# A kernel's planner gets new constants for transfers and a new searched order (block attention and a SoLU layer, one core)

## The chip, the cores and the metric

The kernel runs on one core of one Trainium2 chip. Its engines are TensorE (PE, with a weight-load row PEld), VectorE (DVE), ScalarE (ACT), GpSimd (POOL) and SyncE (SP), which here only issues transfers. Times are device microseconds of one execution; lower is better. An engine executes its own instructions strictly in the order in which the program lists them, each after the semaphores that it needs.

## The reference

Four batches, eight heads, 768 positions, head size 64. Attention runs over a local band of keys and, beside it, over the maxima of blocks of 32 keys; the values are the rows and the block means. Its result goes, as 3072 rows of 512, into a layer with a SoLU and a norm.

```python
k_sum = k.reshape(B, H, nb, 32, D).max(axis=3)
v_sum = v.reshape(B, H, nb, 32, D).mean(axis=3)
scores_l = where(|i - j| < 16, scale * q @ k.T, -1e9)
scores_s = scale * q @ k_sum.T + log(32)
a = softmax(concat([scores_l, scores_s]))          # over both
x = (a @ concat([v, v_sum])) as rows of H * D       # 3072 x 512
h = x @ w_in                                        # 3072 x 1024
solu = h * softmax(h)
ln = (solu - mean) / sqrt(var + 1e-6) * g_ln
out = ln @ w_out                                    # 3072 x 512
```

## The kernel before, in words

The work is cut into 24 tiles t of 128 rows. For a tile, `scores` multiplies queries (qt) with copied windows of keys (kw, line 668), VectorE masks and takes maxima, ScalarE takes the exponentials, `values_turn` transposes them (line 723), and `values` multiplies with the value tile vt (line 770), which holds 96 rows of values (`load_v`) and 24 rows of block means (`load_v2` copies them from vsum). The result is split into a rounded part and a rest (xh, xl), so that three fast matmuls give one precise product. The first product with w_in is `first` (line 922) for the first 8 tiles; from tile 8 on `first_two` (line 941) computes two tiles at once from sums of quarters, with fewer matmuls. `solu` follows, and `second_parts` (line 1117) multiplies with w_out into banks o.

Between `solu` and the second product a tile has to be transposed. Tiles 6 to 23 are "far": `send` transposes 32x32 blocks on VectorE into the one buffer tbl (line 1047) and writes them to DRAM (farl<-tbl, line 1051), and `fetch` reads them back in four transfers of 128 KB (lt<-farl, line 1057), which puts the blocks where they belong. `rows_split` then rounds them on ScalarE or VectorE (lh, lines 367 and 368) and takes the rest (ll). All transfers but the stores of the result and a few copies are issued by SyncE, in one queue.

The order of instructions is not written by hand. The code lists over 1,800 operations, each with one or more engines that can do it, a price for each engine, and what it reads and writes. `Plan.order` plays them through: each engine takes the operation that can begin first, by due time where several can, and an operation with an alternative engine goes where it would end sooner. `Plan.issue` first sets the due times, adds the corrections of the table URGENT and the leanings of the table LEANING (which tilt the choice of an engine), and at the end emits the program in the planned order. While TensorE would stand idle before 80 us (FILL), it puts in dummy matmuls of zeros (line 1309). What the planner believes of a transfer is a few constants: it begins 1 us after its issue ends, all transfers queue one after another at the rate RATES, and it is readable LAND (or an operation's own `land`) after its last byte:

```python
                own = o.end + 1.0 + o.nbytes / self.SMALL * 1e-3
                dma += o.nbytes / next(r for t, r in self.RATES if dma <= t) * 1e-3
                o.end = (own if e == "act" else dma) + (0.2 if dma < self.LATE else o.land or self.LAND)
```

A transfer that moves slower than its bytes say is given more bytes: the write of a far tile counts 1.6 times (FARK), and so does the read back. The price of an operation in `op(engine, price, ...)` is what its engine is held for, for a transfer the time of its issue.

Of the kernel before, what the change touches and what calls it, by code (L numbers as in the profile page):

```python
# [20 lines left out]
P = 128  # L21
# [21 lines left out]
NEAR = 6  # L43
FAR_FROM = 6
FARS = 8
FARK = 1.6
FAR_TO = 24
LATER = 20
PAIRED = 8
# [35 lines left out]
class Plan:  # L85
# [4 lines left out]


    RATES = (6.9, 270.0), (30.0, 410.0), (60.0, 365.0), (1e9, 410.0)
    SMALL, LATE = 40.0, 50.0
    LAND = 2.2
    START = 0.7
    COLD, FILL = 6.9, 80.0
    IDLE = 0.22
    WAIT, FAR = 1.5, 200
    DEAR = {"dve": 1.0, "act": 0.3, "pool": 1.0}
    SYNC = 0.16  # L100
    URGENT = {0: -688, 1: -604, 2: -542, 3: -576, 4: -600, 5: -520, 6: -519, 7: -505, 8: -506, 9: -507, 10: -319, 11:
# [34 lines left out]
    LEANING = {88: -1.9, 97: 1.6, 106: 5.6, 112: -6.5, 157: -5.9, 172: 3.6, 229: 0.2, 294: 1.1, 296: 0.5, 305: -5.8,  # L136
# [8 lines left out]

    def __init__(self):
        self.ops, self.rings, self.banks, self.idle, self.slots = [], {}, {}, None, []
# [106 lines left out]
    def order(self):  # L254
# [45 lines left out]
        while len(order) < len(self.ops):  # L300
            t, e, o = min(((x[0], e, x[1]) for e in ready for x in [take(e)] if x),
                          key=lambda x: (x[0], x[2].due), default=(0.0, None, None))
            if o is None:
                return None
            for f in o.can:
                ready[f] = [x for x in ready[f] if x[1] is not o]
            then.pop(e, None)
            if o.then:
                then[e] = o.then
            o.start, o.engine, (o.cost, o.fn) = t, e, o.can[e]  # L310
            o.end = free[e] = t + cost(e, o, t)
            if e == "dve" and o.port:
                held = o.end
            if e == "pool" and o.port:
                lock = o.end
            if o.nbytes:
                dma = max(dma, o.end + 1.0)
                own = o.end + 1.0 + o.nbytes / self.SMALL * 1e-3
                dma += o.nbytes / next(r for t, r in self.RATES if dma <= t) * 1e-3
                o.end = (own if e == "act" else dma) + (0.2 if dma < self.LATE else o.land or self.LAND)  # L320
            order.append(o)
            for u in o.users:
                u.left -= 1
                if not u.left:
                    enter(u)
# [14 lines left out]
def attn_then_solu(ctx: ExitStack, tc: tile.TileContext, q, k, v, vr, vb, w_in, w_out, g_ln, out):  # L340
# [220 lines left out]
    def mean_values_pe(b):  # L561
# [16 lines left out]
        rows = plan.buf(sb, [P, DM], F32, "os", 2, f"vs{b}")  # L578
        op(act, 0.48, lambda: nc.scalar.copy(out=rows.ap, in_=to()), r=[acc], w=[rows])
        for g in range(4):  # L580
            op(act, 0.34, lambda g=g: nc.scalar.dma_start(
                out=y.ap[WIN + 6 * g:WIN + 6 * g + 6, :], in_=rows.ap[32 * g:32 * g + 6, :]),
               r=[rows], w=[(y, g)], nbytes=6 * 2048)

# [21 lines left out]
    def mean_values(b):  # L606

        vsum[b] = y = plan.buf(sb, [P, DM], F32, "vsum", 1, f"vsum{b}")
        for h in range(H):
            x, p0 = vacc[b, h // 4], h % 4 * NB  # L610
            op(sp, 0.43, lambda h=h, x=x, p0=p0: nc.sync.dma_start(
                out=y.ap[WIN:KC, h * D:(h + 1) * D], in_=x.ap[p0:p0 + NB, :]), r=[x], w=[(y, h)], nbytes=NB * 256)

    def load_q(b, g, pairs=None, after=()):
# [12 lines left out]

    def load_v2(b, g):
        x, y = vt[b, g], vsum[b]
        e, cost, queue = (sp, 0.43, nc.sync) if b else (act, 0.8, nc.scalar)  # L630
        return op(e, cost, lambda: queue.dma_start(
            out=x.ap[WIN:KC], in_=y.ap[WIN:KC, :].rearrange("p (o c) -> p o c", o=1).broadcast_to([NB, G, DM])),
            r=[y], w=[(x, 1)], nbytes=NB * 8192)

    def scores(b, g, pp, direct=False, each=False):

# [417 lines left out]
    def fetch(d, to):  # L1054

        for q in range(4):
            op(sp, 0.43, lambda q=q: nc.sync.dma_start(
                out=to.ap[32 * q:32 * q + 32],
                in_=d.ap.rearrange("(i b) (q x) -> q b i x", i=4, q=4)[q]), r=[d], w=[(to, q)], nbytes=int(P * DF * FARK))

    sent = {}

# [82 lines left out]
    for pp in range(NPP):  # L1145
# [1 line left out]
            key_blocks(0, p)  # L1147
        run(scores(0, 0, pp, True, True))
        if pp == 0:
            op(pool, 0.8, selector, w=[sel_b])  # L1150
            mean_values_first(0)
    for i in range(2 * NKC):
        split_w_in(*divmod(i, 2))
# [200 lines left out]
```

## Time and profile before

| | before |
|---|---|
| time, median of 3 runs | 365.95 us (363.23 to 366.72) |
| the profiled execution: its own time | 365.1 us |
| its span, first to last instruction | 363.4 us |
| granted TensorE clock, mean | 0.994 |
| busy: PE, DVE, ACT, POOL | 353.1, 303.3, 274.1, 170.1 us |
| moved by DMA | 68.19 MB |

The execution's own time has 1.7 us outside the span of its instructions. Busy TensorE is not TensorE at its peak: matmuls are pipelined, and a matmul that is slow to start counts as busy.

### The profile page before, as it was taken

The page shows a single profiled execution, that of the slowest core. Times are in us where ns is not written, and L with a number is a line of the kernel's source. Part 1 is how long each engine was busy: PE and PEld are TensorE (multiplying, and loading weights), DVE is VectorE, ACT ScalarE, POOL GpSimd, SP SyncE. Part 2 cuts the span into 40 slices and gives each one's busy share as a digit, 9 for nine tenths or more (in the row PEclk, how much of TensorE's full clock was granted, in tenths as well). Part 3 has the DMA queues.
Part 4 walks back from the last instruction along what each step waited for, and adds up shares of the span by engine and source line. Part 5 has one row for each costly group of instructions (what it writes and reads, how often), then busy time and mean ns, then how long its engine had stood idle before and what let it go on. Part 6 is the DMA issues. An engine that isn't in the chain of part 4 may idle for free.

```text
span 363.4 us, 9364 instructions
## 1 busy us (share of the span) xinstructions
PE 353.1 (97%) x3318; PEld 276.6 (76%) x3318; DVE 303.3 (83%) x965; ACT 274.1 (75%) x800; POOL 170.1 (47%) x304
## 2 busy tenths in 40 slices
PE   8799999899999999999799999999999999999996
PEld 3438667677777888888688888888888878888886
DVE  4989999998989999896799699895899978949530
ACT  4788999868988988898697597893796976745221
POOL 5542532448779786266636265352332114434400
PEclk9999999999999999999899999999999999999999
DMA  7999994155228047357595193394193282154531
GB/s 250 417 416 389 358 407 156 56 175 170 102 88 265 5 138 252 103 175 239 171 365 181 35 293 135 93 340 114 20 294 118 60 282 90 37 187 168 187 117 58
DMA packets 28530, 68.19 MB, mean 188 GB/s; under 512 B 3852, under 2 KB 13324, under 8 KB 26948
## 3 DMA queue, kind: packets, MB, share of 16 engines
q1 hardware_dynamic: 24620, 60.87, 49.5%
q10 hardware_dynamic: 3864, 6.74, 5.2%
q8 instruction: 26, 0.43, 0.5%
q14 instruction: 20, 0.16, 0.2%
HBM read 49.55 MB, written 15.73 MB: 180 GB/s over the span
## 4 chain that ended last, share of the span: by engine, by line
PE 85%; DMA 10%; DVE 2%; SPq 1%; ACT 1%; issue 0%; ACTq 0%
PE o L1117 33%; PE h L922 13%; PE hu L941 11%; PE x L770 6%; PE s L668 6%; PE hl L941 5%; DMA farl<-tbl 4%; PE t L723 4%; DMA st_v<-in_vr 3%; PE hf L941 2%; DMA raw<-in_w_in 2%; DMA lt<-farl 1%; PE vs_ps L555 1%; PE lt L723 1%; DVE tbl L1047 1%; PE x L762 1%
## 5 line engine op out<-in xcount | busy, mean ns | idle before, releaser
L1117 PE MATMUL o<-w,lh 128*128 128x512 f32 (+1 forms) x400 | 128.7, 385 | 0.7 <-DVE he L1012 0.7
L1117 PEld LDWEIGHTS o<-w,lh 128*128 128x128 f32 x400 | 74.1, 188 | 16.2 <-DVE he L1012 0.9
L1117 PE MATMUL o<-w,ll 128*128 128x512 f32 (+1 forms) x200 | 76.2, 381 | 0.0
L695 ACT ACTIVATE e<-e,nm 128x120 f32<-128x120 f32 x192 | 73.7, 392 | 0.0
L922 PE MATMUL h<-w,xh 128*128 128x512 f32 x128 | 44.2, 404 | 0.0
L1117 PEld LDWEIGHTS o<-w,ll 128*128 128x128 f32 x200 | 37.6, 188 | 6.8
L687 DVE CUSTOM_DVE_ANT_0 e<-s,mask 128x120 f32<-128x120 f32 x192 | 40.6, 277 | 0.4 <-PE s L668 0.4
L695 ACT ACTIVATION_READ_ACCUMULATOR e<-e,nm 128x1 f32 x192 | 37.6, 196 | 0.0
L375 POOL TENSOR_TENSOR ll<-lt,lh 128x512 fp32r<-128x512 f32 x16 | 21.7, 1359 | 29.0 <-DVE lh L368 15.1
L1004 ACT ACTIVATE he<-hs,hm 128x512 f32<-128x512 f32 x24 | 17.2, 718 | 18.0 <-DVE hm L994 18.0
L367 ACT CAST lh<-lt 128x512 fp32r<-128x512 f32 x34 | 20.0, 608 | 14.2 <-PE o L1117 10.5
L1031 POOL TENSOR_SCALAR ss<-ss 128x1 f32<-128x1 f32 x24 | 7.7, 322 | 49.2 <-ACT sq L1027 48.7
L922 PEld LDWEIGHTS h<-w,xh 128*128 128x128 f32 x128 | 24.0, 187 | 7.0 <-DVE nmu L1015 0.8
L1047 DVE STREAM_TRANSPOSE tbl<-he 128x1024 f32<-128x1024 f32 x18 | 22.3, 1237 | 8.2 <-DMA farl<-tbl 7.9
L770 PEld LDWEIGHTS x<-at,vt 120*64 120x64 f32 (+1 forms) x768 | 25.1, 142 | 4.6 <-issue 2.7
L770 PE MATMUL x<-at,vt 120*64 120x64 f32 (+1 forms) x768 | 27.2, 228 | 0.0
L1027 ACT ACTIVATE sq<-he 128x1024 bf16<-128x1024 f32 x24 | 25.4, 1057 | 1.6 <-DVE z L701 1.4
L367 ACT COPY at<-t 120x512 f32<-120x512 f32 x40 | 21.3, 590 | 6.8 <-PE t L723 6.8
L369 POOL COPY kw<-ksum 128x192 f32<-128x192 f32 x19 | 8.4, 441 | 36.0 <-PE s L668 33.6
L922 PE MATMUL h<-w,xl 128*128 128x512 f32 x64 | 25.0, 391 | 0.0
L668 PE MATMUL s<-kw,qt 64*64 64x120 f32 x704 | 22.4, 273 | 2.1 <-ACT kw L367 2.1
L374 DVE TENSOR_TENSOR e<-e,z 128x960 f32<-128x960 f32 x20 | 23.4, 1172 | 0.2
(176 smaller groups left out, 851.5 us busy)
## 6 DMA issues: line engine op xcount, KB each, us to landing
vt<-in_v SPq DMA_DIRECT2D x12, 1024.0 KB
farl<-tbl SPq DMA_DIRECT2D x18, 512.0 KB
lt<-farl SPq DMA_DIRECT2D x72, 128.0 KB
kraw<-in_k SPq DMA_DIRECT2D x16, 400.0 KB
out<-os ACTq DMA_DIRECT2D x23, 256.0 KB
qt<-in_q SPq DMA_DIRECT2D x11, 512.0 KB
raw<-in_w_in SPq DMA_DIRECT2D x8, 512.0 KB
raw<-in_w_out SPq DMA_DIRECT2D x8, 512.0 KB
```

Source lines behind the costliest of these rows:

```text
L367: by = {act: lambda: nc.scalar.copy(out=to(), in_=of()), dve: lambda: nc.vector.tensor_copy(out=to(), in_=of()), pool: lambda: nc.gpsimd.t ...
L374: by = {dve: lambda: nc.vector.tensor_tensor(out=to(), in0=a(), in1=b(), op=kind), pool: lambda: nc.gpsimd.tensor_tensor(out=to(), in0=a() ...
L375: pool: lambda: nc.gpsimd.tensor_tensor(out=to(), in0=a(), in1=b(), op=kind)}
L668: nc.tensor.matmul(sc.ap[cu * QT:(cu + 1) * QT, j, c:c + ks.shape[-1]], qs.ap[ds, 2 * pp + i, u * QT:(u + 1) * QT], ks, start=True, stop=True)
L687: nc.vector.tensor_tensor_reduce(out=e.ap[:, n, :], in0=sc.ap[:, j, (2 * i + up) * KC:(2 * i + up + 1) * KC], in1=mask[:, mi, :], scale=-S ...
L695: nc.scalar.activation(out=e.ap[:, n, :], in_=e.ap[:, n, :], func=AF.Exp, bias=nm.ap[:, n:n + 1], scale=-1.0, accum_out=z.ap[:, n:n + 1])
L770: nc.tensor.matmul(xp()[j * D:(j + 1) * D, i, qs], vs.ap[:k, u, cs], at.ap[:k, u % 2, n[j] + u // 2, :], start=not apart, stop=not apart o ...
L922: nc.tensor.matmul(hp.ap, a.ap[:, c, ts], w.ap[:, i], start=(c == 0 and n == 0), stop=(c == NKC - 1 and n == 2))
L941: nc.tensor.matmul(to.ap, operand(y, n)[:, c], w(c).ap(i), start=first and c == 0 and k == 0, stop=c == 1 and k == 2, skip_group_check=True)
L1027: op(act, 1.06, lambda: nc.scalar.activation(out=sq.ap, in_=e.ap, func=AF.Square, accum_out=ss.ap), r=[e], w=[sq, ss])
L1047: op(dve, 1.17, lambda: nc.vector.transpose(out=tb.ap.rearrange("p (q c a) -> p q c a", q=4, a=32), in_=of().rearrange("p (c q a) -> p q c ...
L1117: nc.tensor.matmul(o.ap[:, cols], a.ap[:, f, :], w.ap[:, i, cols], start=(f == 0 and n == 0), stop=(f == NFC - 1 and n == 2))
```

## The change

No operation is added or removed, and no operand is changed: the same operations are planned with other prices and other tables. After it

- the landing constant depends on when the transfer ends: 0.5 us up to 15 us, 1.4 up to 50, 1.9 later, instead of 0.2 up to 50 and 2.2 later; an operation's own `land` now counts at all times;
- the read back of a far tile counts 2.3 times its bytes, instead of 1.6; the write stays at 1.6 with a landing of 0.1;
- the copy of block means into a value tile for batches 1 to 3 holds SyncE 0.86 us and counts four times its bytes, instead of 0.43 and once;
- the sixteen copies vsum<-vacc hold SyncE 0.76 us each instead of 0.43, the four copies vsum<-vs hold ScalarE 0.75 each instead of 0.34;
- the selector on GpSimd is priced 1.6 us instead of 0.8;
- URGENT and LEANING are replaced. They come from a search whose measure is the mean of five replays of the plan, some of them with disturbances.

```diff
-FARK = 1.6
+FARK, BACK = 1.6, 2.3
...
-    SMALL, LATE = 40.0, 50.0
-    LAND = 2.2
+    SMALL = 40.0
+    LANDS = (15.0, 0.5), (50.0, 1.4), (1e9, 1.9)
...
-    URGENT = {0: -688, 1: -604, 2: -542, 3: -576, 4: -600, 5: -520, 6: -519, 7: -505, 8: -506, 9: -507, 10: -319, 11:
...
+    URGENT = {0: -1754, 1: -1655, 2: -1738, 3: -1698, 4: -1638, 5: -1639, 6: -1608, 7: -1510, 8: -1410, 9: -1372, 10:
...
-    LEANING = {88: -1.9, 97: 1.6, 106: 5.6, 112: -6.5, 157: -5.9, 172: 3.6, 229: 0.2, 294: 1.1, 296: 0.5, 305: -5.8,
...
+    LEANING = {81: 0.8, 100: -4.4, 109: -11.8, 172: 24.7, 176: -6.4, 280: -7.8, 294: -11.9, 296: -5.6, 305: -18.3,
...
-                o.end = (own if e == "act" else dma) + (0.2 if dma < self.LATE else o.land or self.LAND)
+                o.end = (own if e == "act" else dma) + (o.land or next(x for t, x in self.LANDS if dma <= t))
...
-            op(act, 0.34, lambda g=g: nc.scalar.dma_start(
+            op(act, 0.75, lambda g=g: nc.scalar.dma_start(
...
-            op(sp, 0.43, lambda h=h, x=x, p0=p0: nc.sync.dma_start(
+            op(sp, 0.76, lambda h=h, x=x, p0=p0: nc.sync.dma_start(
...
-        e, cost, queue = (sp, 0.43, nc.sync) if b else (act, 0.8, nc.scalar)
+        e, cost, queue = (sp, 0.86, nc.sync) if b else (act, 0.8, nc.scalar)
...
-            r=[y], w=[(x, 1)], nbytes=NB * 8192)
+            r=[y], w=[(x, 1)], nbytes=NB * 8192 * (4 if b else 1))
...
-                in_=d.ap.rearrange("(i b) (q x) -> q b i x", i=4, q=4)[q]), r=[d], w=[(to, q)], nbytes=int(P * DF * FARK))
+                in_=d.ap.rearrange("(i b) (q x) -> q b i x", i=4, q=4)[q]), r=[d], w=[(to, q)], nbytes=int(P * DF * BACK))
...
-            op(pool, 0.8, selector, w=[sel_b])
+            op(pool, 1.6, selector, w=[sel_b])
```

## Rows read from the trace of the kernel before

**Rows 1.** The page: the span, and the busy time of each engine with its share of the span and its instructions.

```profile
span 363.4 us, 9364 instructions
PE 353.1 (97%) x3318; PEld 276.6 (76%) x3318; DVE 303.3 (83%) x965; ACT 274.1 (75%) x800; POOL 170.1 (47%) x304
```

**Rows 2.** The table by stretches of 20 us: the stretch and its length, then busy us and instructions of PE, PEld, DVE, ACT, POOL, the granted clock, the share of DMA, GB/s. Of the eight stretches from 180 to 340 us the first and the one in which PE is least busy are shown.

```profile
20.00:40.00 20.00, 20.00 (x237) 13.01 (x236) 18.80 (x56) 17.07 (x48) 6.48 (x15) 1.00 1.03 385
40.00:60.00 20.00, 20.00 (x202) 13.48 (x201) 19.70 (x68) 18.94 (x60) 6.43 (x11) 1.00 0.93 355
60.00:80.00 20.00, 18.97 (x202) 13.97 (x200) 19.63 (x51) 15.53 (x40) 9.00 (x13) 1.00 0.30 87
...
160.00:180.00 20.00, 17.94 (x162) 14.55 (x163) 14.28 (x58) 15.41 (x53) 13.43 (x24) 0.95 0.65 209
180.00:200.00 20.00, 20.00 (x167) 16.79 (x164) 18.77 (x55) 17.50 (x58) 11.05 (x22) 0.96 0.77 269
...
280.00:300.00 20.00, 19.59 (x206) 16.04 (x203) 18.00 (x69) 17.81 (x61) 2.85 (x7) 1.00 0.47 156
```

**Rows 3.** The dummy matmuls alone (line 1309): the first stretch of 20 us and the sum over all stretches in the same table (PE, PEld), and from the list of that line's instructions (min/median/max ns, first and last start) the form that comes last.

```profile
0.00:20.00 20.00, 11.60 (x45) 4.56 (x45) 1.00 0.91 340
...
sum 363.40, PE 17.00 PEld 6.36; mean PE 0.94 PEld 0.35
...
L1309 PE MATMUL x<-zero x8: 379/379/390, 24.2 to 77.0; 128*128 128x512 bf16 x8
```

**Rows 4.** What TensorE waited for: us in total, times, the longest.

```profile
PE s L668 <- ACT kw L367: 2.1, 1, 2.1
PE vs_ps L1309 <- DVE zero L392: 1.2, 1, 1.2
...
PE o L1117 <- DVE he L1012: 0.7, 1, 0.7
PE s L668 <- DMA kraw<-in_k: 0.6, 1, 0.6
PE s L668 <- DMA qt<-in_q: 0.6, 1, 0.6
```

**Rows 5.** The chain of work that ended last, from 140 to 185 us: start, us, what.

```profile
156.06 1.80 PE s L668 x64
157.86 2.04 PE x L770 x64
...
170.16 5.38 DMA lt<-farl
...
176.34 0.74 ACT kw L367
...
177.13 2.58 PE s L668 x64
179.71 2.86 PE x L770 x64
```

**Rows 6.** ScalarE in order of time: start, us, what, and the idle time before it with what ended it.

```profile
175.72 0.62 ACT L367 CAST lh<-lt 128x512 fp32r<-128x512 f32 x1 [1.93 <-DMA lt<-farl]
```

**Rows 7.** The table by stretches, four us at a time, with the columns of rows 2.

```profile
174.00:178.00 4.00, 1.94 (x38) 1.44 (x40) 2.74 (x6) 1.35 (x2) 1.58 (x2) 1.00 0.24 95
178.00:182.00 4.00, 4.00 (x92) 3.70 (x86) 3.99 (x38) 3.72 (x13) 3.67 (x13) 0.57 0.62 167
```

**Rows 8.** SyncE's queue in order of time: start, us, what, how many.

```profile
167.36 0.34 SPq L1057 DMA_DIRECT2D lt<-farl  x1
167.80 0.86 SPq L631 DMA_DIRECT2D vt<-vsum  x1
168.72 2.43 SPq L1057 DMA_DIRECT2D lt<-farl  x3
```

**Rows 9.** The issues that write or read the block means vsum: min/median/max ns of an issue, first and last start.

```profile
L611 SPq DMA_DIRECT2D vsum<-vacc x16: 713/714/807, 148.9 to 230.7; - x16
L631 SPq DMA_DIRECT2D vt<-vsum x9: 790/845/981, 79.0 to 294.5; - x9
L581 ACTq DMA_DIRECT2D vsum<-vs x4: 681/705/729, 64.2 to 73.9; - x4
```

**Rows 10.** GpSimd in order of time: the first and the last of the selector's four instructions.

```profile
4.08 0.53 POOL L414 MEMSET vsum<- 96x512 f32 x1
...
5.47 0.61 POOL L419 TENSOR_SCALAR_AFFINE_SELECT sel<-sel 128x144 f32<-128x144 f32 x1
```

**Rows 11.** ScalarE in order of time: the first instruction that reads a loaded weight.

```profile
4.75 0.68 ACT L458 ACTIVATE cv<-raw 128x512 f32<-128x512 f32 x1 [2.47 <-DMA raw<-in_w_in]
```

**Rows 12.** The chain of work that ended last, from 270 to 310 us: a write of a far tile.

```profile
288.84 7.38 DMA farl<-tbl
```

**Rows 13.** SyncE, VectorE and TensorE in order of time, around that write.

```profile
287.18 1.13 SPq L625 DMA_DIRECT2D vt<-in_v  x1
...
296.24 1.25 DVE L1047 STREAM_TRANSPOSE tbl<-he 128x1024 f32<-128x1024 f32 x1 [1.67 <-DMA farl<-tbl]
...
298.18 0.50 PE L941 MATMUL hu<-ws_v,xl 128*128 128x512 f32 x1 [0.41 <-DVE xl L374]
```

**Rows 14.** What VectorE waited for: us in total, times, the longest.

```profile
DVE tbl L1047 <- DMA farl<-tbl: 7.9, 4, 4.7
```

90 rows, old and new, of tables (LEANING, URGENT) are left out of this document.

## The prediction, made before the change was run

> **What bounds the kernel now.** I read the engines' shares and the 40 slices first [rows 1]. TensorE is busy 353.1 of 363.4 us, VectorE 303.3, the DMA engines about half of the time. So the end is set by TensorE's instruction stream, and the program on every engine is the same before and after except for its order: only a wait that TensorE sees, or a dummy matmul that fills one, can change the time. The table by stretches [rows 2] shows where such waits lie. From 20 to 80 us TensorE counts as busy, but VectorE is busy 18.8, 19.7 and 19.6 of each 20 us, so that stage is VectorE's; from 180 to 340 us TensorE is never idle over 0.41 us in 20. One stretch stands out, 160 to 180: TensorE 17.94 of 20 us, and there and in the next stretch the mean granted clock is 0.95 and 0.96. The dummy matmuls [rows 3] are 17.0 us of what counts as busy, 11.6 of them in the first 20 us, under the first loads.
>
> The list of waits of TensorE [rows 4] says what a better order can win: 2.1 us behind one copy of key windows, and nothing else of more than 1.2 us. The chain of waits around it [rows 5] tells why. The first of the four reads that bring one tile's transposed rows back (lt<-farl) is issued at 167.36, the last at 170.16, and the last lands at 175.54. ScalarE's queue has the rounding of those rows (lh) ahead of the copy kw, ScalarE stands 1.93 us on the landing [rows 6], kw comes behind it, and the scores that need kw start at 177.13. [...] The price of that: 64 scores take 2.58 us in the chain instead of 1.80, 64 value products 2.86 instead of 2.04 [rows 5], together 1.6 us. The whole accident costs 2.1 + 1.6 = **3.7 us**.
>
> **The constants, one by one.** None is executed; each makes the planner place work later or earlier.
> - The read back, the factor in bytes from 1.6 to 2.3, the landing after 50 us from 2.2 to 1.9 us, and the copy of block means into the value tile from 192 KB and 0.43 us of issue to four times the bytes and 0.86. I work out what the planner held of the accident, from the issue at 167.36 in the trace. SyncE issues read, vt<-vsum, read, read, read [rows 8]. Old: five issues of 0.43 end at 169.51; the transfer begins 1.0 later, takes 128 KB x 1.6 / 410 GB/s = 0.51 and lands 2.2 later: 173.2. New: the issues end at 169.94; the transfers queue, 0.74 from 168.79, then 192 KB x 4 / 410 = 1.92, then three of 0.74, to 173.8; landing 1.9 later: 175.7. The trace has 175.54 [rows 5]. The planner of before held the rows landed 2.3 us too early, which is the size of the stall, and the new one is right to 0.2 us. The median issue of vt<-vsum is 845 ns [rows 9], so 0.86 is right too.
> - The issue of the sixteen vsum<-vacc on SyncE from 0.43 to 0.76 us: 714 ns in the trace; that of the four vsum<-vs on ScalarE from 0.34 to 0.75: 705 ns [rows 9]. The latter four were 4 x 0.37 = 1.5 us of ScalarE's time that the plan didn't have, in the stage from 64 to 74 us; TensorE's idle 0.7 us behind the solu product he [rows 4] lies in it.
> - The selector on GpSimd from 0.8 to 1.6: its four instructions run from 4.08 to 6.08 us [rows 10]. The change is worth 0 to 0.8 us, its size; I take 0, since TensorE's list of waits [rows 4] has none on the selector.
> - The landing of early loads from 0.2 to 0.5 us (to 15 us) and 1.4 (to 50). The first load: 0.7 + 0.43 + 1.0 + 512 KB / 270 GB/s = 4.07, so landed and seen at 4.4 by the old value and 4.7 by the new (0.16 for the semaphore); ScalarE starts on it at 4.75 [rows 11].
>
> All constants go toward the trace, so the plan is believable where it was not. What it does with it is in the new tables of due times and leanings, which no row of before shows. Nor is the position of any instruction after the change known.
>
> **The sum.** The accident: -3.7 us where it goes wholly, -2.1 where only the idle goes and the clock would have stayed up; I take -3.7, since the profiled run shows both parts. What becomes late next is another reader of a far tile; TensorE's list of waits has none behind one but this [rows 4]. The rest of the plan: -1.6 us if the 60 to 80 us stage (1.0 idle, [rows 2]) and half of the waits on first loads (1.2 of kraw and qt, [rows 4]) go, 1.6; +1.6 if the order gives up as much in the stretches that lose 0 to 0.4 us now. I take -0.2, near nothing, as VectorE's load in the stage to 80 us doesn't change. Against the profiled execution of 365.1 us that is 361.2. The median of the timed runs is 0.85 above that execution, so **362.05, say 362.0**.
>
> **Rivals.**
> - *The clock alone.* [...] In a run where it had stayed up, the accident costs 2.1 and its removal gives 365.95 - 2.1 - 0.2 = **363.6**. For it: the times spread from 363.23 to 366.72, more than the 1.6. Against: the profiled execution has the fall and is faster than the median. [...]
> - *The stall moves.* The search puts another late wait of the same kind in a place that was tight. ScalarE's and VectorE's queues are in order, and 16 of the 18 far tiles go through one buffer lt. Price again 3.7 for one: **365.9**, no change. For it: every due time is new, the search follows a mean of five replays and not this chip; from 180 us on the order of before is nearly without loss, so new positions can only lose there.
> - *The write that the plan still doesn't see.* The write farl<-tbl keeps factor 1.6 and a landing of 0.1. In the trace it takes 7.38 us from 288.84 [rows 12]; the planner, with 1 MB of vt<-in_v ahead from 287.18 [rows 13], has 287.61 + 1.0 + 2.56, a read of 0.51 and 2.05 for itself, 0.1 landing: 293.8 against 296.21, 2.4 too early (2.2 by the new factor). VectorE's next transposition waits for it, since tbl has one buffer: 7.9 us in four waits, the longest 4.7 [rows 14]. The 1.67 us wait at 296.24 cost TensorE 0.41 [rows 13], so some 1.3 us are covered. Where the new order sets a wait beyond that ahead of the splits xl that TensorE needs, the rest is paid one to one, and the clock on top: 3.7 us at a wait of 3.4. One of these gives 365.8; from the second on the kernel is slower: 362.05 + 2 x 3.7 = **369.5** (368 to 373).
> - *VectorE's stage gets shorter.* The new leanings move work from VectorE to GpSimd, which is busy 6.5 and 6.4 of 20 us from 20 to 60 [rows 2]. If half of the 5.4 us of dummies after 20 us [rows 3] goes and 0.8 of small losses with it: 362.05 - 3.5, **358.5**. Against: the planner prices a subtraction at 1.26 us on GpSimd and 0.6 on VectorE (LO_W), which no constant changes, and the old tables had the same freedom.
> - *It does not do what it says* would need constants that miss the trace. They don't, as shown above.
>
> **How the numbers follow.** Forecast 0.38 (359.5 to 363.3 around 362.0), clock alone 0.10, the stall moves 0.24 (364 to 367.5), the write 0.18, VectorE's stage 0.10. What measurement can tell from no change is 1%, 362.3 to 369.6. Faster by more: 0.29 of the forecast's 0.38 and 0.10 of the shorter stage, 0.39. Same: 0.09 + 0.10 + 0.24 + 0.05 of the write, 0.48. Slower: 0.13. The range 358.5 to 369.0 leaves out some 0.07 below and 0.12 above; the forecast's own is 359.5 to 363.3.
>
> **What would show it.** Right: the profile after has no TensorE idle behind a kw copy of 2 us, a granted clock of 1.00 in every stretch from 20 to 340 us, and ScalarE waits on lt<-farl under 1 us; TensorE's dummies stay near 17 us. The clock rival: the times of before fall in two groups. The stall moves: a stretch other than 160 to 200 us with TensorE under 19 of 20 us and a clock under 1. The write: VectorE's wait tbl <- farl<-tbl above 12 us in sum, with TensorE waiting on xl. The shorter stage: dummies below 14.5 us, and the last of them earlier than 77.0 us [rows 3]. The forecast is wrong if the stretches from 180 us on lose more than 2 us together, which no row of before would have told.

## The result and the profile after

The changed kernel takes 367.43 us in the median (365.83 to 368.39), the kernel before, measured beside it, 365.11 us (363.19 to 367.40): a ratio of 1.0055 [1.0034, 1.0077]. The change costs 2.0 us. The profiled execution of after took 368.39 us, the slowest of its twenty. The ratios leave out executions more than 1.5% above the fastest of their kernel: two of before, and two each of the new front with the old rest and of the new order up to 150 us, whose medians below are without them. All lines are six further down than before, so the scores are L674 and the dummies L1315.

The page of after, first lines, to be read against [rows 1]:

```profile
span 366.6 us, 9384 instructions
...
PE 355.9 (97%) x3325; PEld 277.3 (76%) x3330; DVE 299.1 (82%) x953; ACT 273.6 (75%) x800; POOL 181.1 (49%) x316
```

VectorE has 4.2 us less to do and GpSimd 11.0 us more: the new plan did move work, and the time did not fall. TensorE's 7 more matmuls are dummies. What TensorE waited for (us in total, times, the longest):

```profile
PE s L674 <- DMA qt<-in_q: 1.8, 2, 1.5
PE s L674 <- DVE ll L1101: 1.7, 1, 1.7
```

and VectorE's wait behind the write of a far tile, in its own list:

```profile
DVE tbl L1053 <- DMA farl<-tbl: 1.3, 1, 1.3
```

The wait behind a copy kw [rows 4] is gone, and so is every wait of ScalarE on lt<-farl [rows 6]; the wait behind the write fell from 7.9 [rows 14] to 1.3 us. A new wait of 1.7 us stands behind the rest ll of another tile. (The 1.8 us behind qt lie before 15 us, under the first loads; the table of losses below has no more lost up to 60 us than before.) The table by stretches of 20 us shows where (columns as in [rows 2]):

```profile
60.00:80.00 20.00, 19.45 (x177) 13.57 (x176) 18.89 (x53) 15.38 (x46) 8.25 (x8) 1.00 0.16 48
80.00:100.00 20.00, 18.52 (x193) 14.62 (x195) 16.55 (x55) 16.32 (x44) 13.15 (x27) 0.91 0.47 142
...
160.00:180.00 20.00, 20.00 (x204) 16.47 (x204) 17.38 (x63) 18.76 (x59) 9.12 (x19) 1.00 0.74 229
```

From 160 to 180 us TensorE is busy 20.00 us at a clock of 1.00, where it was 17.94 at 0.95. The loss is now at 80 us. And 60 to 80 only looks better than before (19.45 against 18.97): the same table for the dummies alone, after and then before, says why.

```profile
60.00:80.00 20.00, 4.39 (x18) 1.70 (x19) 1.00 0.16 48
```

```profile
60.00:80.00 20.00, 1.00 (x3) 0.21 (x3) 1.00 0.30 87
```

4.39 us of what counts as busy there are matmuls of zeros, 3.4 us more than before. The chain of work that ended last shows both holes (start, us, what):

```profile
64.54 0.34 DVE cv L485
64.88 0.12 DVE z L707
...
65.14 1.80 POOL e L381
66.94 0.04 issue
66.98 0.70 PE t L729 x16
67.69 0.02 issue
67.71 0.60 ACT at L373
...
70.42 1.86 DVE w L504 x2
...
78.71 0.72 ACT he L1030
79.43 0.48 ACT lh L373
79.91 0.02 issue
79.93 1.30 DVE ll L1101 x2
81.23 0.25 issue
81.48 1.05 PE s L674 x32
```

The first hole: the reciprocal z of a softmax stands behind VectorE's masks and a conversion, its product e x z runs on GpSimd in 1.80 us, and only then can TensorE transpose. The planner foresaw this one and filled it. The second hole, 79.74 to 81.48, was not planned, so nothing fills it: VectorE, in the chain from 68 us on with one short turn over ScalarE, comes to ll late. TensorE in order of time (start, us, what, idle before and what ended it):

```profile
63.49 3.41 PE L1315 MATMUL x<-zero 128*128 128x512 bf16 x14
66.98 0.69 PE L729 MATMUL t<-ident,e 64*120 64x64 f32 x16
67.60 1.04 PE L1315 MATMUL x<-zero 128*128 128x512 bf16 x4
...
81.48 1.05 PE L674 MATMUL s<-kw,qt 64*64 64x120 f32 x32 [1.73 <-DVE ll L1101]
```

Behind the second hole the granted clock falls (stretches of four us, columns as in [rows 2]):

```profile
78.00:82.00 4.00, 2.27 (x42) 1.69 (x44) 3.67 (x8) 3.48 (x9) 0.34 (x1) 1.00 0.85 217
82.00:86.00 4.00, 4.00 (x44) 2.81 (x35) 3.82 (x22) 3.34 (x13) 3.16 (x5) 0.58 0.14 32
```

0.58 is mostly a lower level of 0.50, which each us from 83 to 86 us has: the same picture as in [rows 7] at another place, where each us from 179 to 181 has 0.50.

To add this up, take every useful matmul of the trace at the time that it has back to back at a granted clock of 1.00 (from start to start 0.227 us for 512 columns, 0.028 for a score); this work, an estimate, is 321.6 us in each order. What a stretch has beyond it is lost there, whether by idle time, dummies, slow starts or the clock:

| lost, us | before | after | old front, new rest (below) |
|---|---|---|---|
| 0 to 60 us | 22.6 | 22.4 | 23.3 |
| 60 to 90 | 4.1 | 9.8 | 4.1 |
| 90 to 170 | 3.8 | 5.1 | 4.0 |
| 170 to 180 | 3.6 | 0.3 | 0.6 |
| 180 to 230 | 1.4 | 2.2 | 1.7 |
| 230 to the end | 6.2 | 5.2 | 5.1 |

The accident is repaired (3.3 us), and the new order pays 5.7 us between 60 and 90, and 1.3 between 90 and 170. Some 1.5 us of the 5.7 is the low clock: the trace of the new front with the old rest (below), which has the same two holes and a granted clock of 1.00 behind them, by the same count loses that much less from 60 to 90.

### The profile page after: what moved, and what is told of

The parts are those of the page before. It is cut to its first block, busy times and chain, and to the rows that moved or that the text cites. A ratio compares the mean times of both kernels' runs of the same rounds, so it can differ in the third digit from the quotient of the medians.

```text
span 366.6 us, 9384 instructions
## 1 busy us (share of the span) xinstructions
PE 355.9 (97%) x3325; PEld 277.3 (76%) x3330; DVE 299.1 (82%) x953; ACT 273.6 (75%) x800; POOL 181.1 (49%) x316
## 4 chain that ended last, share of the span: by engine, by line
PE 66%; DVE 18%; ACT 6%; DMA 5%; issue 2%; SPq 1%; POOL 0%; ACTq 0%; DVEq 0%; POOLq 0%
PE o L1123 30%; PE hu L947 10%; PE hl L947 5%; PE x L776 4%; PE h L928 4%; PE s L674 4%; PE hf L947 3%; DMA qt<-in_q 3%; DVE e L693 3%; PE t L729 3%; ACT e L701 2%; DMA farl<-tbl 2%; DVE he L1018 2%; PE vs_ps L561 1%; DVE hm L1005 1%
## 5 line engine op out<-in xcount | busy, mean ns | idle before, releaser
L373 ACT CAST lh<-lt 128x512 fp32r<-128x512 f32 x39 | 22.8, 608 | 11.3 <-PE o L1123 8.8
L1030 ACT ACTIVATE he<-he,nmu 128x512 f32<-128x512 f32 x32 | 22.6, 722 | 10.6 <-DVE nmu L1021 10.5
L381 POOL TENSOR_TENSOR xl<-sums,xh 128x256 fp32r<-128x256 f32 (+1 forms) x18 | 15.8, 880 | 26.4 <-ACT xh L373 23.9
L381 POOL TENSOR_TENSOR ll<-lt,lh 128x512 fp32r<-128x512 f32 x13 | 18.3, 1411 | 12.8 <-ACT lh L373 9.6
L674 PE MATMUL s<-kw,qt 64*64 64x120 f32 x704 | 21.7, 267 | 1.8 <-DVE ll L1101 1.7
```

The source lines that it names most:

```text
L373: by = {act: lambda: nc.scalar.copy(out=to(), in_=of()), dve: lambda: nc.vector.tensor_copy(out=to(), in_=of()), pool: lambda: nc.gpsimd.t ...
L381: pool: lambda: nc.gpsimd.tensor_tensor(out=to(), in0=a(), in1=b(), op=kind)}
L674: nc.tensor.matmul(sc.ap[cu * QT:(cu + 1) * QT, j, c:c + ks.shape[-1]], qs.ap[ds, 2 * pp + i, u * QT:(u + 1) * QT], ks, start=True, stop=True)
L1030: (act, 0.62, lambda sl=sl: nc.scalar.activation(out=e.ap[:, sl], in_=e.ap[:, sl], func=AF.Identity, bias=nmu.ap))], port=True)
```

## Experiments

Since the planner plays everything anew for any edit, single moves were made in its result. The order is given as a list, a letter for the engine (p TensorE, a ScalarE, v VectorE, g GpSimd, s SyncE) and the number of the operation, and the planner's arithmetic then runs along the list; before's own list gives before's program. In a fixed order the constants of that arithmetic set only the dummies; they are those of before in the lists that begin as before does (but for the last one, "searched on"), and those of after in the others. Each edit is in this line and in the list (the lists of the mixed orders are written as they were made):

```diff
-        order = self.order()
+        order = fixed(self)
```

**The copy kw ahead of the landing.** Before's list; on ScalarE the copy (939) goes ahead of the rounding lh (989).

```diff
 p885 g773
+a939
 a989 v991 v992 p891
-a939
 g990 p886
```

> The order of before with one step moved: on ScalarE the copy of key windows kw goes ahead of the rounding lh that waits for the rows read back. Theory (the accident is this one queue position and costs 2.1 us of idle and 1.6 us of low clock): 3.7 us less than before, some 361.4 us, and no granted clock under 1 from 20 to 340 us. Rival (only the idle is won, the clock is lost elsewhere): 2.1 us less, 363.0. Rival (the next reader of the far tile takes the place, the second product that needs lh): less than 1 us won, 364.5 to 365.5, with TensorE waiting on lh or ll instead.

Measured: 364.88 against 364.43 us, ratio 1.0002 [0.9968, 1.0036]: a gain of 1.2 us at most, where the sum had 2.1 to 3.7. The wait on kw is gone from the list. VectorE's queue stands on the same landing, and what TensorE needs from it comes late; VectorE and ScalarE, then TensorE in order of time:

```profile
177.38 0.43 DVE L368 CAST lh<-lt 128x512 fp32r<-128x512 f32 x1 [1.26 <-DMA lt<-farl]
...
177.37 0.62 ACT L367 CAST lh<-lt 128x512 fp32r<-128x512 f32 x1 [1.24 <-DMA lt<-farl]
...
190.90 0.50 PE L1117 MATMUL o<-w,lh 128*128 128x512 f32 x1 [1.54 <-DVE os L1125]
```

**Every queue past the landing.** On top of that, all that reads these rows (the roundings and rests 989 to 992, and the next read into their buffer, 993) goes behind VectorE's maxima hm of the other tile (901), so that no queue should stand on them.

```diff
+a939
-a989 v991 v992
 p891
-a939 g990
 ...
-s993
 g757 v901
+a989 g990 v991 v992 s993
```

> The order of before, with the wait for the rows read back taken out of both queues at 175 us: on ScalarE the copy kw and on VectorE the two additions hs and the maximum hm go ahead of the rounding lh and the rest ll. Moving kw alone gave nothing, and there VectorE stood on the same landing. Theory (the accident costs what both queues stand): 2 to 3 us under before, 362 to 363. Rival (the rows are late for the second product and for the next tile's buffer lt, whatever the queues do; only another order of the far tiles wins the time): within 0.8 us of before, the planner with the new constants has 353.9 against 353.7.

Measured: 365.30 against 364.05 us, ratio 1.0020 [0.9995, 1.0045]. Again nothing. TensorE has 20.00 of 20 us busy from 160 to 180 and then waits; VectorE, then TensorE:

```profile
174.17 0.69 DVE L368 COPY at<-t 120x512 f32<-120x512 f32 x1 [2.52 <-ACT at L367]
...
176.27 0.42 DVE L368 CAST lh<-lt 128x512 fp32r<-128x512 f32 x1
176.72 1.77 DVE L374 TENSOR_TENSOR ll<-lt,lh 128x512 fp32r<-128x512 f32 x1
...
189.42 0.50 PE L1117 MATMUL o<-w,lh 128*128 128x512 f32 x1 [1.50 <-DVE os L1125]
```

So the place of lh in a queue was the form of the stall, not its whole cause. ScalarE still stands 1.11 us on the landing here, but VectorE rounds the rows without waiting for them, and TensorE waits for VectorE all the same. What VectorE had lost by then is the 2.52 us at 174.17, for a copy `at` of ScalarE; from there to os, which ends at 189.4, the chain of work that ended last is almost all VectorE's. Before has the same wait ahead of the accident:

```profile
173.82 0.69 DVE L368 COPY at<-t 120x512 f32<-120x512 f32 x1 [2.53 <-ACT at L367]
```

In the order of the next experiment no idle time of VectorE from 150 to 190 us is over 0.65 us. No run takes this one wait away alone, so it is read from the traces and not shown by an edit.

**Old front, new rest.** What before plans ahead of 150 us in before's order, all that is left in after's.

```diff
+order = [x for x in before_list if before_start[x] < 150] + [x for x in after_list if not taken]
```

> The order of before for all operations that it plans ahead of 150 us, and all others in the order of after. Theory (the loss of the change lies in its first 90 us, and the rest of the new order is the better one): the first 90 us lose as before and the rest loses 2.2 us less than before, 363 us, 0.4 to 0.7% under before, and 4 us under after. Rival (the loss is spread over the whole new order): 366 to 368.

Measured: 361.48 us (361.07 to 362.12) against 364.43, ratio 0.9912 [0.9880, 0.9944]: 3.2 us faster than before, and the fastest order here. Its stretches and then its longest waits of TensorE:

```profile
160.00:180.00 20.00, 20.00 (x169) 15.76 (x168) 17.73 (x61) 16.52 (x57) 12.19 (x23) 1.00 0.78 253
180.00:200.00 20.00, 20.00 (x191) 16.56 (x184) 17.47 (x65) 17.05 (x56) 14.10 (x24) 1.00 0.80 264
```

```profile
PE vs_ps L1309 <- DVE zero L392: 1.2, 1, 1.2
PE s L668 <- DVE ksum L535: 1.1, 1, 1.1
```

Here is the gain that the prediction looked for, with the clock at 1.00 in all six executions. It comes with the new order of the whole rest, not with one moved copy.

**New front, old rest.** The reverse, cut at 100 us of after's plan.

```diff
+order = [x for x in after_list if after_start[x] < 100] + [x for x in before_list if not taken]
```

> The order of after for all operations that it plans ahead of 100 us, and all others in the order of before, with the accident on ScalarE's queue. Theory (the loss lies in the first 90 us): 5.4 us over before, 370 us, 1.3 to 1.6% slower, with both the stall at 80 us and that at 175 us, and two stretches of low clock. Rival (what the front loses is made up later): 365 to 367.

Measured: 367.53 against 364.43 us, ratio 1.0083 [1.0049, 1.0117], 3.0 us slower. Both stalls, the new and the old, are in its list of waits, the old one with 0.8 us instead of 2.1:

```profile
PE s L674 <- DVE ll L1101: 1.7, 1, 1.7
...
PE s L674 <- ACT kw L373: 0.8, 1, 0.8
```

The clock did not fall behind the new stall in this execution:

```profile
80.00:100.00 20.00, 18.54 (x215) 14.96 (x216) 17.87 (x66) 17.71 (x48) 14.44 (x31) 1.00 0.54 165
```

**The middle, twice.** After's order up to 150 us and before's rest; then before's up to 100 and after's rest.

```diff
+order = [x for x in after_list if after_start[x] < 150] + [x for x in before_list if not taken]
```

```diff
+order = [x for x in before_list if before_start[x] < 100] + [x for x in after_list if not taken]
```

> The order of after for all operations that it plans ahead of 150 us, the others in the order of before. It differs from the new front to 100 us by the stretch from 100 to 150 us alone. The three runs so far don't add up: front +3.0, rest -3.2, and the whole +2.0. Theory (the stretch from 100 to 150 us of the new order loses the missing 2.2): 5.2 over before, 369.6. Rival (the stretches are innocent, the late front makes the rest of the new order lose, which the old rest takes better): 367 to 368, as the new front to 100 us.

> The order of before for all operations that it plans ahead of 100 us, the others in the order of after. Against the old front to 150 us it has the new stretch from 100 to 150 us instead of the old one. Theory (that stretch of the new order costs about 2 us whatever stands ahead of it, as with the new front): 363 to 364.5, of which the seam at 105 to 110 us has 1.4 of planned idle against 0.6 of the seam at 159. Rival (it costs only behind the late new front): 361.5 to 362.3.

Measured: the first 368.70 against 364.78 us, ratio 1.0132 [1.0090, 1.0174], by the ratios 1.8 us more than with the cut at 100, by the medians 0.8, and the two intervals overlap. The second 363.50 against 364.05, ratio 0.9975 [0.9951, 0.9999], a gain of 0.9 us where the cut at 150 gained 3.2; these intervals do not overlap. So the new order from 100 to 150 costs something behind either front. Two stretches of the second, where the old order has 20.00 us busy in each, and then the first of them in after:

```profile
100.00:120.00 20.00, 19.42 (x179) 15.20 (x178) 18.53 (x62) 16.56 (x58) 15.09 (x22) 1.00 0.51 163
...
140.00:160.00 20.00, 19.53 (x188) 15.20 (x186) 17.55 (x56) 17.50 (x46) 10.90 (x20) 1.00 0.46 154
```

```profile
100.00:120.00 20.00, 20.00 (x215) 15.78 (x211) 18.58 (x68) 15.08 (x53) 16.37 (x27) 1.00 0.46 150
```

After loses nothing to idle time there: the 0.58 us of the mixed order belongs to its seam at 100, while the loss at 140 to 160 is in after too (19.53). A mixed order pays for its seam as well, and 1.8 to 2.3 us is more than the 1.3 us that the table has for 90 to 170. What the seams take was not measured by itself.

**The two products, there and back.** The product e x z of two tiles runs in 1.16 us on VectorE before and in 1.79 on GpSimd after. In before's list both go to GpSimd; in after's both go to VectorE, behind their reciprocals.

```diff
-v258 ... v323
+g258 ... g323
```

```diff
-g258 v314 ... v300 ... g323
+v258 v314 ... v323 v300 ...
```

> The order of before, with the two products e times 1/z that after does on GpSimd between 60 and 75 us moved there too (before has them on VectorE, 1.16 us each). Theory (the choice of engine makes the hole in the front): each of the two makes TensorE wait 0.6 us longer, 1.79 instead of 1.16, and GpSimd slows VectorE's roundings beside it; 1.3 to 3 us over before. The planner with the new constants has 1.2 more. Rival (the hole comes from the place in the queue, not from the engine): under 1 us more.

> The order of after, with the same two products moved from GpSimd to VectorE, right behind the reciprocals that they read. Theory (engine choice): the hole of 3.4 us at 64 us and the stall at 80 us shrink, 1.3 to 3 us under after, 364.5 to 366. Rival (VectorE bounds this stage, and in this order it has no room): no gain, or 2 us over after, as the planner has it (354.2 instead of 352.2).

Measured: before with the products on GpSimd 365.82 against 364.78 us, ratio 1.0028 [1.0001, 1.0056], 1.0 us slower. After with the products on VectorE 366.88 us, ratio to before 1.0067 [1.0042, 1.0092], no better than after itself. VectorE in order of time tells why the second product off VectorE frees nothing. After: two weight products (w) beside GpSimd's product, and that product; then the same two with the product on VectorE:

```profile
70.34 2.54 DVE L504 SCALAR_TENSOR_TENSOR w<-cv,g_sb,w 128x512 fp32r<-128x512 f32 x2
...
69.88 1.79 POOL L381 TENSOR_TENSOR e<-e,z 128x960 f32<-128x960 f32 x1 [0.51 <-DVE z L707]
```

```profile
70.58 1.15 DVE L380 TENSOR_TENSOR e<-e,z 128x960 f32<-128x960 f32 x1
71.65 1.41 DVE L504 SCALAR_TENSOR_TENSOR w<-cv,g_sb,w 128x512 fp32r<-128x512 f32 x2
```

The pair takes 1.13 us longer beside GpSimd, and the product that VectorE was spared is 1.15 us. The first product does free VectorE, whose two reductions beside it take 1.75 us (0.94 for one elsewhere in the trace); but TensorE's transposition then starts at 66.98 instead of 66.29, and VectorE stands 0.78 us at 68.33 for what comes of it. Before with the products on GpSimd (VectorE, and GpSimd's product beside it), and below it the same pair before:

```profile
62.42 2.82 DVE L466 TENSOR_SCALAR cv<-raw 128x512 int32<-128x512 int32 x2
...
62.23 1.93 POOL L375 TENSOR_TENSOR e<-e,z 128x960 f32<-128x960 f32 x1 [6.43 <-DVE hm L1001]
```

```profile
63.38 0.75 DVE L466 TENSOR_SCALAR cv<-raw 128x512 int32<-128x512 int32 x2
```

With the products on VectorE, the plan sees the hole at 80 us and fills it; TensorE in order of time:

```profile
80.11 1.47 PE L1315 MATMUL x<-zero 128*128 128x512 bf16 x5
81.66 1.05 PE L674 MATMUL s<-kw,qt 64*64 64x120 f32 x32
```

The clock stays up in all six executions, yet the scores start at 81.66, no earlier than the 81.48 of after. The hole is there as in after, filled instead of empty: the engine of the two products does not make it. That the new order's sequence on VectorE does is read from the chain above.

**The new constants with the old tables.** All constants of the change, URGENT and LEANING as before; a single execution.

```diff
-    URGENT = {0: -1754, 1: -1655, 2: -1738, ...
+    URGENT = {0: -688, 1: -604, 2: -542, ...
```

> All the new constants, with the old tables URGENT and LEANING. If the constants alone were what makes the plan better, 361 to 365 us. Theory (the tables are corrections to one course of planning, by the number of the operation, and a changed price sends the planning another way): far slower; the planner itself ends TensorE at 380.9 us instead of 348.8, and by the distance of before (16.3 us from the planned end of TensorE to the time) that is 397 us.

Measured: 392.32 us, 25 us slower than the new tables with the same constants. TensorE's list of waits begins with a product on GpSimd:

```profile
PE t L723 <- POOL e L375: 8.5, 1, 8.5
```

The old tables do not hold with the new constants; the new tables with the old constants were not run. So tables and constants can't be judged apart in this way, and the mixed orders above had to serve.

**Searched on.** From the old front and new rest, a search by single moves on the planner's own measure (the new constants, with the old ones and dearer prices beside them). With the new constants it brings the planned end of TensorE from 351.6 to 349.6 us.

```diff
-old_front_list
+list after single moves, each kept where the planned end came earlier
```

> From the old front with the new rest (361.5 us) searched on by single moves, with the planner's own replay under the new constants (and the old, and with prices up to 8% higher) as the measure: the planned end of TensorE goes from 351.6 to 349.6. If the new constants are true in steps of 2 us, 359.5. [...]

Measured: 366.03 against 364.78 us, ratio 1.0035 [1.0012, 1.0058]. 2.0 us better in the plan is 4.5 us worse on the chip (1.3 slower than before, after 3.2 faster). Its longest wait, 1.9 us of it at 98.66:

```profile
PE h L928 <- DVE he L1018: 2.6, 2, 1.9
```

## Why the prediction was wrong

The prediction said 362.0 us, about 1% faster; the kernel became 2 us slower, inside the range.

- *Read rightly: the accident and its repair.* No wait behind kw, TensorE full from 160 to 180 us, no wait of ScalarE on the rows. The new rest gives 3.2 us (by its interval 2.0 to 4.4) against the 3.7 of the sum. But its explanation was too narrow: the prediction had the queue position of lh as the cause, and two moves of just this gained nothing.
- *The clock in that term was mis-sized.* 1.6 of the 3.7 us was the granted clock (0.57 from 178 to 182 us [rows 7]), and the profiled execution that showed it was not a typical one. Of 67 executions of before, 19 have a mean clock of 0.996 or less, and their median is 366.1 us against 364.1 of the others. These are the two groups that the clock rival asked for, though they overlap (365.4 to 368.1, 362.7 to 366.3), and where the clock fell is known of the profiled one alone. Against the others the new rest gains 2.6 us (364.1 to 361.5). One and the same order has the fall in some executions and not in others: after has such a mean clock in 10 of 20 (367.9 against 366.2 us).
- *The step that failed: "the rest of the plan", -0.2, bounded by ±1.6.* It came out at about +5: +3.0 for the front up to 100 us, +1.8 to +2.3 from 100 to 150 (seams included; the 1.8 is 0.8 by the medians). With -3.2 for the rest this makes +1.6 to +2.1, and +2.0 was measured. Taken from the other side, against after, the front is +2.9 (before up to 100, after's rest) and the rest -2.8 (after up to 150, before's rest); each of these figures is uncertain by 1 to 2 us. The bound was taken from what before still lost in these stretches and from VectorE's load, which "doesn't change". The load even fell, 18.89 against 19.63 of 20 us from 60 to 80. What decided here is which of VectorE's results came when: VectorE was as good as full in either order, and in the new one its z and its ll came late for TensorE.
- *The rival that came nearest: "the stall moves".* Its mark was a stretch outside 160 to 200 us with TensorE under 19 of 20 us and a clock under 1; that is 80 to 100 with 18.52 and 0.91. But it named a far tile's landing as the next stall and a price of 3.7 (which makes 365.75 by its own terms, not 365.9). It was VectorE's own lateness, beside a hole that the plan knew of and a dearer middle, and together these cost more than the repair gave.
- *The other rivals.* The write's wait became small (1.3 us). Dummies went to 19.2 us, not below 14.5, so VectorE's stage became no shorter. That the constants miss the trace is not borne out by the rows that the prediction gave for them, nor did the stretches from 180 on lose more than before (7.4 against 7.6 in the table).

That the constants fit the trace of before was true of those for which the prediction had a row, and the step from there to "the plan is believable" was not. Played along before's list, the new constants have TensorE end 5.0 us later than the old ones do (353.7 against 348.75), for the same program. By them the new order is 1.5 us better than the old (352.16); by the old constants it is 3.0 us worse (351.76), and the chip says 2.0 worse. The mixed orders say more. The planner's arithmetic, run along their lists, is right about one half with each set: for the new front with the old rest the old constants give 2.4 us more than for before's list and the new ones 0.3 (measured 3.0), for the old front with the new rest the old ones give 0.3 more and the new ones 2.1 less (measured 3.2 less). In that arithmetic two of the changed constants hide the price of the new front: the landings up to 50 us and the issue of vsum<-vs at 0.75 us, put into the old set, bring its 2.4 down to 0.2, and the new set without these two gives 2.5 for the front and 2.1 less for the rest. Both go toward their rows [rows 9], [rows 11]. Why the chip does not pay in the old front what they say is open, and no tables were searched without them.

## What to carry to other kernels

A corrected price repairs the place that it was wrong for; a search over the whole order deals every other stretch anew, and a stretch that ran well can then only lose. Keep the part of the order that the trace shows without loss, and plan only the rest again: here this turned a loss of 2.0 us into a gain of 3.2. A step in the plan smaller than its error on the chip (here 2.0 us better planned was 4.5 us worse) is no step until it is measured.

## What the runs showed of the hardware

VectorE slows down beside GpSimd on these operations: two products with two tensor operands took 2.54 instead of 1.41 us, and two integer operations 2.82 instead of 0.75, while GpSimd's products beside them took 1.79 and 1.93 us; so that a product of 1.16 us moved to GpSimd was paid back on VectorE. Not every operation was slowed: two reductions beside such a product took 1.75 us (0.94 for one elsewhere in the trace). The first pair, begun at 70.34, had 1.33 us to the end of GpSimd's product at 71.67, and lost 1.13; the second, begun at 62.42, had 1.74 to the end of the product beside it at 64.16, and lost 2.07. So each lost about what was left of the product, to 0.2 and 0.3 us; by what mechanism, no run shows.

And idle times of TensorE of about 2 us (2.06 before [rows 7], 1.73 after) were followed by a granted clock of 0.57 and 0.58 over four us, mostly 0.50, in the profiled executions. A mean clock of 0.996 or less is seen in a part of the executions only, 19 of 67 and 10 of 20, and these took 2.0 and 1.6 us longer in the median (before, after). The trace of the new front with the old rest has the same wait of 1.7 us and the clock at 1.00. In the four orders in whose traces TensorE has no wait over 1.2 us after the first 20 us (the old front with the new rest, the old order up to 100 us, and the two with the products moved), 1 of 36 executions has a mean clock that low.
